# Moving the split of p' w_in from VectorE to ScalarE and GpSimd, from the third batch on

## The chip, the cores and the metric

The kernel runs on one core of a Trainium2 chip. Its engines each follow their own queue of instructions: TensorE (PE in the profile; its weight loads are PEld), VectorE (DVE), ScalarE (ACT), GpSimd (POOL) and SyncE (SP), which here issues the transfers. The metric is the time on the device in microseconds (us). Three runs of the kernel before took 813.12, 812.82 and 815.71 us; the median is 813.12 us.

## The reference

Eight batches of 576 tokens with 8 heads of 64 go through a packed attention, and its output through a feed-forward network (FFN) with a leaky activation, all in float32:

```python
p_packed = sm_attn(p, k, v)                # 32 packed rows per head
out = sm_attn(q, p_packed, p_packed)       # softmax over the 32 packed rows
x = out.transpose(0, 2, 1, 3).reshape(B * S, H * D)
h = x @ w_in                               # (4608, 512) x (512, 2048)
g = np.maximum(h, 0.0) + alpha * np.minimum(h, 0.0)
return g @ w_out                           # (4608, 2048) x (2048, 512)
```

## The kernel before

The attention's output is A times the packed rows p', where A holds the softmax weights of 32 packed rows for each of 8 heads, 256 columns in all. So x w_in is A (p' w_in), and the kernel never forms x: for each batch it computes p' w_in once (256 x 2048) and multiplies A with it. That product is the tile `pw`, kept in float32 in four pieces of 512 columns for each batch.

TensorE multiplies fp32r, a rounded float32. To keep the precision the kernel splits an operand in two: a high part, which is the value cast to fp32r, and a low part, which is the value less the high part, cast too. A product is then three matmuls: high by high, low by high, and high by low.

The FFN goes over half-batches k (288 tokens, two for each batch) and over f, 16 slices of 128 of the 2048 hidden columns. One step is a call of `first` and a call of `second`, two steps apart:

- `first(k, f)` multiplies two halves of `pw` with A into `ps_h` in PSUM (lines 639, 640, 641: high by high, high by A's low part, low by high: six matmuls), and then runs a chain of four small operations: `neg` on ScalarE (645), the leaky sum into `ps_h` on VectorE (646), `gh`, the high part, on ScalarE (651), `gl`, the low part, on VectorE (652).
- `second(k, f)` multiplies `gh` and `gl` with w_out into four accumulators `acc` (669, 670, 671: twelve matmuls).

`split_pw(k, h)` (lines 606 to 616) makes the high part `pwh` and the low part `pwl` of 256 columns of `pw`, which serve two steps f. They have two buffers each. It is called anew for each half-batch, so eight times for each k; k from 2 on needs it (k 0 and 1 go another way), which makes 14 times 8, or 112 calls. For k 2 and 3 (the second batch) ScalarE casts, from k 4 on (the third batch) VectorE casts; VectorE subtracts in all of them.

Beside the FFN of two batches the attention of the next two runs, and then their p' w_in (lines 595 to 597, copied to `pw` at 600, with the split w_in loaded at 567 into `w`, which has three buffers). In the attention GpSimd has the low parts of k and q (`xl`, 180), of v (`vs`, 309, one buffer) and of A (`a_l`, 455), and two steps of the second softmax (431, 438). ScalarE has their high parts (179, 308, 454).

The order of each engine's queue is not written out: a scheduler with its own estimate of every duration sorts the instructions when the kernel is built, and each engine then works through its queue strictly in that order.

Of the kernel before, what the change touches and what calls it, by code (L numbers as in the profile page):

```python
# [13 lines left out]
ALU = mybir.AluOpType  # L14
# [8 lines left out]
def fv(ap):  # L23

    return ap.bitcast(F32)
# [3 lines left out]
def pack_attention_ffn_kernel(  # L29
# [20 lines left out]
    nc = tc.nc  # L50
# [24 lines left out]
    op = ctx.enter_context(tc.tile_pool(name="op", bufs=4))  # L75
# [530 lines left out]
    def split_pw(k, h):  # L606

        src = pw[k // 2, h // 2][:, :, (h % 2) * 256 : (h % 2) * 256 + 256]
        th = pwj.tile([P, 2, 256], F32R, name="pwh", tag="pwh")
        tl = pwj.tile([P, 2, 256], F32R, name="pwl", tag="pwl")  # L610
        if k < 4:
            nc.scalar.copy(out=th, in_=src)  # L612
        else:
            nc.vector.tensor_copy(out=th, in_=src)  # L614
        nc.vector.tensor_tensor(out=tl, in0=src, in1=fv(th), op=ALU.subtract)  # L615
        pj[k, h] = (th, tl)

    def first(k, f):
# [4 lines left out]
        if k < 2 * XF:  # L623
            th, a_f = pw[k // 2, f // 4], result[k // 2]
            fs = slice((f % 4) * P, (f % 4) * P + P)
            for i in range(2):
                nc.tensor.matmul(  # L627
                    ps[:, :HS], th[:, i, fs], a_f[:, i, tok], start=(i == 0), stop=(i == 1)
                )
        else:  # L630
            a_h, a_l = result[k // 2]
            key = (k, f // 2)
            if key not in pj:
                split_pw(*key)
            th, tl = pj[key]
            fs = slice((f % 2) * P, (f % 2) * P + P)
            for i in range(2):
                hi, lo = (i == 0), (i == 1)
                nc.tensor.matmul(ps[:, :HS], th[:, i, fs], a_h[:, i, tok], start=hi, stop=False)  # L639
                nc.tensor.matmul(ps[:, :HS], th[:, i, fs], a_l[:, i, tok], start=False, stop=False)  # L640
                nc.tensor.matmul(ps[:, :HS], tl[:, i, fs], a_h[:, i, tok], start=False, stop=lo)  # L641
# [181 lines left out]
```

## Time and profile before

| what | value |
|---|---|
| median of three runs | 813.12 us |
| the profiled execution | 815.99 us, of it 813.9 us span |
| PE busy | 774.5 us (95%) |
| DVE busy | 611.6 us (75%) |
| ACT busy | 495.1 us (61%) |
| POOL busy | 186.5 us (23%) |
| `pwl` on DVE, line 615, 112 times | 89.9 us, 802 ns each |
| `pwh` on DVE, line 614, 96 times | 53.9 us, 562 ns each |
| `pwh` on ACT, line 612, 16 times | 9.9 us, 618 ns each |

The span is the time from the first to the last instruction of one profiled execution; the execution took 2.1 us more than its span. Busy time of PE counts overlapping matmuls once, so 95% does not say that TensorE had to wait for the other 5% alone. What an engine waits for is named by the semaphore that came last. The chain that ended last goes back from the last instruction, at each step to what released it.

### The profile page before, as it was taken

The page shows a single profiled execution, that of the slowest core. Times are in us where ns is not written, and L with a number is a line of the kernel's source. Part 1 is how long each engine was busy: PE and PEld are TensorE (multiplying, and loading weights), DVE is VectorE, ACT ScalarE, POOL GpSimd, SP SyncE. Part 2 cuts the span into 40 slices and gives each one's busy share as a digit, 9 for nine tenths or more (in the row PEclk, how much of TensorE's full clock was granted, in tenths as well). Part 3 has the DMA queues.
Part 4 walks back from the last instruction along what each step waited for, and adds up shares of the span by engine and source line. Part 5 has one row for each costly group of instructions (what it writes and reads, how often), then busy time and mean ns, then how long its engine had stood idle before and what let it go on. Part 6 is the DMA issues. An engine that isn't in the chain of part 4 may idle for free.

```text
span 813.9 us, 14922 instructions
## 1 busy us (share of the span) xinstructions
PE 774.5 (95%) x5376; PEld 731.0 (90%) x5376; DVE 611.6 (75%) x1302; ACT 495.1 (61%) x1162; POOL 186.5 (23%) x195
## 2 busy tenths in 40 slices
PE   5789999999989899999999999999999999999997
PEld 4557678989989799998999999999999999999997
DVE  4999799778877567899886487898975466666664
ACT  5788898777766676565657655566557533333332
POOL 2101312225436113354342012444311000000000
PEclk9979999999999999999999999999999999999999
DMA  9977787322414743222227522321007200000000
GB/s 298 375 240 241 265 288 246 111 62 59 126 53 128 262 150 97 75 67 66 63 74 230 200 59 59 89 59 45 2 26 260 81 31 1 31 1 30 1 30 30
DMA packets 58457, 93.77 MB, mean 115 GB/s; under 512 B 5136, under 2 KB 36880, under 8 KB 58384
## 3 DMA queue, kind: packets, MB, share of 16 engines
q1 hardware_dynamic: 58384, 92.83, 35.0%
q8 instruction: 42, 0.69, 0.3%
q14 instruction: 31, 0.25, 0.1%
HBM read 72.88 MB, written 19.92 MB: 114 GB/s over the span
## 4 chain that ended last, share of the span: by engine, by line
PE 76%; DVE 9%; DMA 5%; ACT 4%; issue 1%; ACTq 0%; SPq 0%; DVEq 0%
PE acc L669 15%; PE acc L670 14%; PE acc L671 14%; PE ps_h L639 6%; PE ps_h L640 6%; PE ps_h L641 6%; DMA w<-w_split 3%; PE ps_h L627 3%; PE ps_m L595 1%; PE ps_m L216 1%; PE ps_m L597 1%; PE ps_m L596 1%; PE ps_m L217 1%; PE ps_m L350 1%; DVE pwl L615 1%
## 5 line engine op out<-in xcount | busy, mean ns | idle before, releaser
L669 PE MATMUL acc<-gh,wo 128*128 128x288 f32 x1024 | 287.9, 301 | 9.2 <-ACT gh L651 8.2
L670 PE MATMUL acc<-gh,wo 128*128 128x288 f32 x1024 | 282.9, 296 | 0.0
L669 PEld LDWEIGHTS acc<-gh,wo 128*128 128x128 f32 x1024 | 193.0, 189 | 16.3 <-ACT gh L651 12.3
L671 PE MATMUL acc<-gl,wo 128*128 128x288 f32 x1024 | 198.0, 299 | 0.0
L670 PEld LDWEIGHTS acc<-gh,wo 128*128 128x128 f32 x1024 | 193.2, 189 | 1.7 <-issue 0.2
L651 ACT CAST gh<-ps_h 128x288 fp32r<-128x288 f32 x256 | 102.0, 400 | 124.6 <-DVE ps_h L646 122.7
L652 DVE TENSOR_TENSOR gl<-ps_h,gh 128x288 fp32r<-128x288 f32 x256 | 115.5, 453 | 71.8 <-ACT gh L651 70.4
L645 ACT ACTIVATE neg<-ps_h 128x288 f32<-128x288 f32 x256 | 105.4, 412 | 99.5 <-PE ps_h L641 89.5
L646 DVE SCALAR_TENSOR_TENSOR ps_h<-neg,nal,ps_h 128x288 f32<-128x288 f32 x256 | 131.3, 515 | 46.1 <-ACT neg L645 45.5
L671 PEld LDWEIGHTS acc<-gl,wo 128*128 128x128 f32 x1024 | 157.0, 188 | 2.6
L639 PE MATMUL ps_h<-a_h,pwh 128*128 128x288 f32 x448 | 134.2, 300 | 3.4 <-DVE gl L652 3.3
L640 PE MATMUL ps_h<-a_l,pwh 128*128 128x288 f32 x448 | 132.2, 295 | 0.0
L641 PE MATMUL ps_h<-a_h,pwl 128*128 128x288 f32 x448 | 131.9, 295 | 0.0
L180 POOL TENSOR_TENSOR xl<-xraw,xh 128x576 fp32r<-128x576 f32 x48 | 70.0, 1460 | 200.4 <-ACT xh L179 185.8
L615 DVE TENSOR_TENSOR pwl<-pw,pwh 128x512 fp32r<-128x512 f32 x112 | 89.9, 802 | 9.4 <-ACT pwh L612 3.5
L639 PEld LDWEIGHTS ps_h<-a_h,pwh 128*128 128x128 f32 x448 | 84.2, 188 | 6.0 <-DVE gl L652 5.0
L640 PEld LDWEIGHTS ps_h<-a_l,pwh 128*128 128x128 f32 x448 | 84.3, 188 | 0.5
L641 PEld LDWEIGHTS ps_h<-a_h,pwl 128*128 128x128 f32 x448 | 84.2, 188 | 0.1
L600 ACT COPY pw<-ps_m 64x512 f32<-64x512 f32 x120 | 69.6, 580 | 18.5 <-PE ps_m L597 16.6
L614 DVE CAST pwh<-pw 128x512 fp32r<-128x512 f32 x96 | 53.9, 562 | 24.1 <-PE ps_h L640 23.7
L309 POOL TENSOR_TENSOR vs<-vraw,vs 128x640 fp32r<-128x640 f32 x24 | 38.8, 1616 | 40.3 <-ACT vs L308 38.7
L219 ACT COPY lo<-ps_m 64x288 f32<-64x288 f32 x96 | 37.6, 396 | 9.4 <-PE ps_m L217 7.3
(128 smaller groups left out, 987.8 us busy)
## 6 DMA issues: line engine op xcount, KB each, us to landing
w<-w_split SPq DMA_DIRECT2D x48, 512.0 KB, 3.9
xraw<-in_kT SPq DMA_DIRECT2D x32, 288.0 KB, 3.0
xraw<-in_qT SPq DMA_DIRECT2D x32, 288.0 KB, 2.8
outT<-ot SPq DMA_DIRECT2D x64, 144.0 KB, 2.2
vraw<-in_v SPq DMA_DIRECT2D x32, 256.0 KB, 3.0
wraw<-in_w_in SPq DMA_DIRECT2D x16, 512.0 KB, 5.8
wraw<-in_w_out SPq DMA_DIRECT2D x16, 512.0 KB, 4.9
w_split<-w SPq DMA_DIRECT2D x16, 512.0 KB, 3.6
```

What stands on the lines that cost most here:

```text
L180: nc.gpsimd.tensor_tensor(out=xl, in0=raw, in1=fv(xh), op=ALU.subtract)
L615: nc.vector.tensor_tensor(out=tl, in0=src, in1=fv(th), op=ALU.subtract)
L639: nc.tensor.matmul(ps[:, :HS], th[:, i, fs], a_h[:, i, tok], start=hi, stop=False)
L640: nc.tensor.matmul(ps[:, :HS], th[:, i, fs], a_l[:, i, tok], start=False, stop=False)
L641: nc.tensor.matmul(ps[:, :HS], tl[:, i, fs], a_h[:, i, tok], start=False, stop=lo)
L645: nc.scalar.activation(out=neg, in_=x, func=AF.Relu, scale=-1.0)
L646: nc.vector.scalar_tensor_tensor(out=x, in0=neg, scalar=nal[:, f : f + 1], in1=x, op0=ALU.mult, op1=ALU.add)
L651: nc.scalar.copy(out=gh, in_=x)
L652: nc.vector.tensor_tensor(out=gl, in0=x, in1=fv(gh), op=ALU.subtract)
L669: nc.tensor.matmul(acc[o][:, :HS], wo_t[f][:, 0, os_], gh, start=begin, stop=False)
L670: nc.tensor.matmul(acc[o][:, :HS], wo_t[f][:, 1, os_], gh, start=False, stop=False)
L671: nc.tensor.matmul(acc[o][:, :HS], wo_t[f][:, 0, os_], gl, start=False, stop=end)
```

## The change

From k 4 on the cast to `pwh` runs on ScalarE, as it did for k below 4, and the subtraction to `pwl` on GpSimd. VectorE keeps the subtraction for k 2 and 3 alone. Ninety-six casts and 96 subtractions leave VectorE's queue.

```diff
@@ split_pw
-        if k < 4:
-            nc.scalar.copy(out=th, in_=src)
-        else:
-            nc.vector.tensor_copy(out=th, in_=src)
-        nc.vector.tensor_tensor(out=tl, in0=src, in1=fv(th), op=ALU.subtract)
+        nc.scalar.copy(out=th, in_=src)
+        low = nc.vector if k < 4 else nc.gpsimd
+        low.tensor_tensor(out=tl, in0=src, in1=fv(th), op=ALU.subtract)
         pj[k, h] = (th, tl)
```

The file is two lines shorter, so lines from 615 on have numbers lower by two in the rows of the change (646 becomes 644); its cast is line 611 and its subtraction 613. The scheduler sorted all queues anew. Up to the first split of the third batch nothing moved. Three places behind it matter for the prediction. A number behind a name tells the tiles of one name apart.

**First place**, about 408 us into the span, VectorE's queue in the fourth batch's FFN. `s2` and `c` belong to the attention. Before:

```order
L453 STREAM_TRANSPOSE s2_4579<-t1_4693 128x576
L652 TENSOR_TENSOR gl_5601<-ps_h_5586,gh_5600 128x288
L359 TENSOR_TENSOR c_4789<-ps_m_4790,ct_4796 128x128
L614 CAST pwh_5699<-pw_3145 128x512
L615 TENSOR_TENSOR pwl_5700<-pw_3145,pwh_5699 128x512
L646 SCALAR_TENSOR_TENSOR ps_h_5616<-neg_5623,nal_107,ps_h_5616 128x288
L652 TENSOR_TENSOR gl_5627<-ps_h_5616,gh_5626 128x288
```

Now:

```order
L650 TENSOR_TENSOR gl_5601<-ps_h_5586,gh_5600 128x288
L436 TENSOR_SCALAR z2_4744<-z2_4744 128x18
L437 RECIPROCAL z2_4744<-z2_4744 128x18
L644 SCALAR_TENSOR_TENSOR ps_h_5616<-neg_5623,nal_107,ps_h_5616 128x288
L359 TENSOR_TENSOR c_4789<-ps_m_4790,ct_4796 128x128
L650 TENSOR_TENSOR gl_5627<-ps_h_5616,gh_5626 128x288
L644 SCALAR_TENSOR_TENSOR ps_h_5642<-neg_5653,nal_107,ps_h_5642 128x288
L453 STREAM_TRANSPOSE s2_4579<-t1_4693 128x576
```

Nothing of the split stands between two steps of the FFN's chain any more, and the attention's transpose has gone two steps back. ScalarE's queue at the same place, before:

```order
L651 CAST gh_5600<-ps_h_5586 128x288
L358 COPY ct_4796<-ps_m_4790 128x128
L308 CAST vs_4799<-vraw_4724 128x5x128
L454 CAST a_h_4822<-s2_4579 128x576
L645 ACTIVATE neg_5623<-ps_h_5616 128x288
L651 CAST gh_5626<-ps_h_5616 128x288
```

Now:

```order
L649 CAST gh_5600<-ps_h_5586 128x288
L611 CAST pwh_5699<-pw_3145 128x512
L643 ACTIVATE neg_5623<-ps_h_5616 128x288
L358 COPY ct_4796<-ps_m_4790 128x128
L308 CAST vs_4799<-vraw_4724 128x5x128
L649 CAST gh_5626<-ps_h_5616 128x288
```

The cast of the split stands right ahead of `neg`.

**Second place**, about 529 us, GpSimd's queue in the fifth batch's FFN, at the k and q of the next attention. Before:

```order
L438 TENSOR_TENSOR t1_6782<-t1_6782,z2_6831 128x576
L409 CAST pt_110<-p2_109 128x2x64 x2
L180 TENSOR_TENSOR xl_6850<-xraw_6680,xh_6849 128x576
L455 TENSOR_TENSOR a_l_6866<-s2_6663,a_h_6865 128x576
L180 TENSOR_TENSOR xl_7125<-xraw_7017,xh_7124 128x576
```

Now:

```order
L438 TENSOR_TENSOR t1_6782<-t1_6782,z2_6831 128x576
L613 TENSOR_TENSOR pwl_7414<-pw_5328,pwh_7413 128x512
L188 MEMSET vraw_7259 64x128
L409 CAST pt_110<-p2_109 128x2x64 x2
L455 TENSOR_TENSOR a_l_6866<-s2_6663,a_h_6865 128x576
L180 TENSOR_TENSOR xl_6850<-xraw_6680,xh_6849 128x576
L613 TENSOR_TENSOR pwl_7488<-pw_5328,pwh_7487 128x512
L180 TENSOR_TENSOR xl_7125<-xraw_7017,xh_7124 128x576
```

`xl_6850` has moved behind a `pwl` and behind `a_l`. TensorE's queue where it is read, before:

```order
L671 MATMUL acc3_7131<-gl_7215,wo4_558 128x288
L216 MATMUL ps_m_6876<-xh_6849,s1_108 128x288
L217 MATMUL ps_m_6870<-xl_6850,s1_108 128x288
L217 MATMUL ps_m_6876<-xl_6850,s1_108 128x288
L669 MATMUL acc0_7128<-gh_7273,wo5_658 128x288
```

Now:

```order
L669 MATMUL acc3_7131<-gl_7331,wo6_725 128x288
L216 MATMUL ps_m_6876<-xh_6849,s1_108 128x288
L217 MATMUL ps_m_6870<-xl_6850,s1_108 128x288
L217 MATMUL ps_m_6876<-xl_6850,s1_108 128x288
L667 MATMUL acc0_7128<-gh_7367,wo7_938 128x288
```

The reader has moved too: from behind f 4 (`wo4`) to behind f 6 (`wo6`), two steps of the FFN later.

**Third place**, about 270 us, SyncE's queue at the start of the third batch's FFN. `w` is a piece of the split w_in, `outT` a part of the output. Before:

```order
L567 DMA w_3378<-w_split_100 128x1024
L567 DMA w_3398<-w_split_100 128x1024
L687 DMA outT<-ot_3579 128x288
L687 DMA outT<-ot_3585 128x288
L567 DMA w_3450<-w_split_100 128x1024
```

Now:

```order
L567 DMA w_3378<-w_split_100 128x1024
L685 DMA outT<-ot_3579 128x288
L685 DMA outT<-ot_3585 128x288
L567 DMA w_3398<-w_split_100 128x1024
L685 DMA outT<-ot_3591 128x288
L567 DMA w_3450<-w_split_100 128x1024
```

Two writes of the output have moved ahead of the load of `w_3398`.

## The prediction

> **What bounds the kernel now.** I read the busy time of each engine first, then the same by stages, then who TensorE waits for, and last the chain of waits at the places where it stood still.
>
> ```profile
> span 813.9 us, 14922 instructions
> PE 774.5 (95%) x5376; PEld 731.0 (90%) x5376; DVE 611.6 (75%) x1302; ACT 495.1 (61%) x1162; POOL 186.5 (23%) x195
> ```
>
> The stages, with PE, PEld, DVE, ACT and POOL busy, their instructions, the granted clock, and the transfers:
>
> ```profile
> 268.00:281.00 13.00, 9.67 (x49) 8.50 (x50) 7.77 (x15) 8.49 (x17) 1.45 (x2) 0.91 0.84 274
> 345.00:380.00 35.00, 32.87 (x242) 31.79 (x241) 33.09 (x65) 21.17 (x52) 16.21 (x16) 1.00 0.23 69
> 405.00:415.00 10.00, 8.87 (x69) 8.73 (x68) 8.51 (x17) 4.78 (x12) 4.74 (x5) 1.00 0.11 31
> 495.00:535.00 40.00, 38.46 (x283) 36.97 (x282) 34.25 (x72) 23.38 (x59) 16.39 (x17) 1.00 0.23 68
> 281.00:780.00 499.00, 493.05 (x3611) 483.55 (x3610) 365.17 (x762) 273.96 (x651) 104.67 (x97) 1.00 0.24 76
> 720.00:780.00 60.00, 60.00 (x456) 60.00 (x454) 38.87 (x80) 21.88 (x55) 0.00 (x0) 1.00 0.06 21
> ```
>
> TensorE is the bound. From 720 to 780 us it never stops: 60.00 us for 456 matmuls is 132 ns each, and a step of 18 matmuls takes 2.37 us. The first changed split starts at about 268 us, so nothing before that can move. From 281 to 780 us TensorE stands idle for 499.00 - 493.05 = 5.95 us, of it 2.13 us in 345 to 380, 1.13 in 405 to 415 and 1.54 in 495 to 535: 4.80 us in three stretches where VectorE is 95%, 85% and 86% busy. That is nearly all that a lighter VectorE can give back. Whom TensorE waited for between 281 and 780 us (total us, times, longest one):
>
> ```profile
> PE acc L669 <- ACT gh L651: 3.3, 4, 1.1
> PE ps_m L595 <- DMA w<-w_split: 1.2, 2, 0.7
> PE acc L669 <- DVE ot L685: 0.7, 2, 0.4
> PE ps_m L216 <- DVE p L385: 0.5, 1, 0.5
> PE ps_h L639 <- DVE gl L652: 0.3, 1, 0.3
> ```
>
> All but the transfer's 1.2 us end with the FFN's chain or VectorE: 8 waits, 4.8 us. The name `gh` is ScalarE's, but ScalarE was late because VectorE was. The chain that ended last shows it at 408 us (start, us, what), and at 530 us likewise:
>
> ```profile
> 409.26 1.57 DVE pwh L614
> ...
> 410.93 1.73 DVE pwl L615
> 412.65 0.44 DVE ps_h L646
> ...
> 413.12 0.41 ACT gh L651
> ...
> 413.57 0.40 PE acc L669
> ```
>
> ```profile
> 529.89 1.67 DVE pwh L614
> ```
>
> At 408 us the split alone holds the chain for 3.3 us. A cast of 1.57 or 1.67 us is not what it usually costs. GpSimd at the same time:
>
> ```profile
> 408.97 1.57 POOL L309 TENSOR_TENSOR vs<-vraw,vs 128x640 fp32r<-128x640 f32 x1 [1.06 <-ACT vs L308]
> 410.50 1.61 POOL L455 TENSOR_TENSOR a_l<-s,a_h 128x576 fp32r<-128x576 f32 x1
> ```
>
> VectorE's cast ends just after GpSimd's first subtraction does (410.83 and 410.54), and `pwl` just after the second (412.66 and 412.11). They hold each other up.
>
> **The change part by part.** VectorE's groups between 281 and 814 us (busy us, mean ns, then idle before and what ended it), with ScalarE's and GpSimd's groups nearest to the new operations, from 60 us on:
>
> ```profile
> L646 DVE SCALAR_TENSOR_TENSOR ps_h<-neg,nal,ps_h 128x288 f32<-128x288 f32 x190 | 97.6, 516 | 41.7 <-ACT neg L645 41.3
> L615 DVE TENSOR_TENSOR pwl<-pw,pwh 128x512 fp32r<-128x512 f32 x93 | 74.3, 798 | 5.7 <-PE ps_h L641 0.4
> L614 DVE CAST pwh<-pw 128x512 fp32r<-128x512 f32 x93 | 52.7, 567 | 24.1 <-PE ps_h L640 23.7
> L612 ACT CAST pwh<-pw 128x512 fp32r<-128x512 f32 x16 | 9.9, 618 | 3.7 <-PE ps_h L640 3.6
> L180 POOL TENSOR_TENSOR xl<-xraw,xh 128x576 fp32r<-128x576 f32 x48 | 70.0, 1460 | 200.4 <-ACT xh L179 185.8 <-PE ps_h L640 9.5 <-PE ps_h L641 2.8
> L309 POOL TENSOR_TENSOR vs<-vraw,vs 128x640 fp32r<-128x640 f32 x24 | 38.8, 1616 | 40.3 <-ACT vs L308 38.7 <-PE ps_h L627 1.0 <-PE acc L671 0.6
> ```
>
> *Removed.* VectorE loses 52.7 + 74.3 = 127 us, so its 365 us between 281 and 780 become some 240 of 499: half busy. What that is worth is not 127 us but the waits of TensorE. By the three stretches it is 4.80 us; since a matmul is busy for 295 ns but a new one starts every 132, each of the 8 waits hides another 0.16 us, and the ceiling is 4.80 + 8 x 0.16 = 6.1 us. At 408 us the split was 3.3 us of a chain that came 1.1 us late, so without it the wait is gone. I take four fifths for what is really regained, since the order is new and some waits will stand elsewhere: **-4.9 us**. The bounds are nothing and -6.1.
>
> *Added to ScalarE.* 93 casts of 618 ns are 57 us, so 274 us of 499 become 331, or 66%. The cast stands ahead of `neg` and waits, as VectorE's did, until `ps_h`'s second high matmul (640) has freed the buffer. What that does is seen in the steady stage, where a split falls into every second step:
>
> ```profile
> 743.79 0.43 DVE L614 CAST pwh<-pw 128x512 fp32r<-128x512 f32 x1 [0.42 <-PE ps_h L640]
> 744.33 0.69 DVE L615 TENSOR_TENSOR pwl<-pw,pwh 128x512 fp32r<-128x512 f32 x1
> 744.94 0.52 DVE L646 SCALAR_TENSOR_TENSOR ps_h<-neg,nal,ps_h 128x288 f32<-128x288 f32 x1
> 743.99 0.41 ACT L645 ACTIVATE neg<-ps_h 128x288 f32<-128x288 f32 x1 [1.11 <-PE ps_h L641]
> 745.49 0.40 ACT L651 CAST gh<-ps_h 128x288 fp32r<-128x288 f32 x1 [1.08 <-DVE ps_h L646]
> 746.64 0.30 PE L669 MATMUL acc<-gh,wo 128*128 128x288 f32 x1
> ```
>
> Before, `neg` was done at 744.40 and `ps_h` still waited for `pwl` until 744.94. Now the cast ends at 743.79 + 0.62 = 744.41, `neg` at 744.82, and `ps_h` can start at 744.86: 0.08 us earlier. `gh` is needed at 746.64 and was there at 745.89. So in the steady stage the cast costs **nothing**, hidden by the slack of 0.75 us; were that slack gone, each cast would cost up to 0.45 us of lateness of `neg`. Beside the attention, where ScalarE has long casts too, I charge +0.2 us.
>
> *Added to GpSimd.* No row has 128x512 there. From 1460 ns for 576 columns and 1616 for 640, 64 columns are worth 156 ns, and 512 take about 1.30 us; the bounds are VectorE's undisturbed 0.69 (row at 744.33) and 1.46. 93 of them are 121 us, so 105 us of 499 become 226, or 45%. They are covered by time: a split made at 743.79 takes the buffer that one pair of steps just freed and serves the pair after the running one, two steps or 4.7 us later. Cast and subtraction took 0.43 + 0.69 = 1.1 us and now take 0.62 + 1.30 = 1.9, which leaves 2.8 us, room for one long subtraction of the attention ahead in GpSimd's queue and not for two.
>
> *GpSimd's own work made later.* `xl_6850` now waits behind a `pwl` and `a_l` (second place in the order), about 1.3 + 1.6 us. Its reader on TensorE has been moved back by two steps, 4.7 us. I charge nothing.
>
> *What VectorE still shares with GpSimd.* The tiny scalar operation on `z` swings likewise (ns, least, median, most):
>
> ```profile
> L436 DVE TENSOR_SCALAR z<-z x16: 127/168/1398, 32.3 to 612.1; 128x18 f32<-128x18 f32 x16
> ```
>
> `ps_h`, which reads PSUM, takes 516 ns in the mean and 0.52 us in the steady stage with GpSimd idle, so it is not held. With GpSimd busy twice as long, `z` meets it more often: 8 of them after 281 us at up to 1.2 us more each, of which TensorE sees a part: +0.5 us, between 0 and 2. The Trainium skill (SBUF — State Buffer, "Who interferes with whom") says that a two-input VectorE operation on SBUF and the faster modes of copies and scalar operations exclude a GpSimd operation for its whole length, whichever starts first; the trace agrees in the casts of 1.57 and 1.67 us. By that rule the removed operations are the very ones that were held, so all 6.1 us would come back, and the sum would be -4.9 us.
>
> *Transfers.* At the third place `w_3398` is now issued behind two output writes. It is what TensorE waits for there:
>
> ```profile
> 271.90 5.65 DMA w<-w_split
> ```
>
> ```profile
> 272.32 0.86 SPq L687 DMA_DIRECT2D outT<-ot  x2
> ```
>
> The stage 268 to 281 lost 13.00 - 9.67 = 3.3 us so. The two writes took 0.86 us to issue and were ready before, so the load goes out at most that much later, and less where they no longer wait behind it: +0.5 us, between 0 and 0.9.
>
> The sum is -4.9 + 0.2 + 0.5 + 0.5 = **-3.7 us**. The profiled execution took 815.99 us (813.9 span and 2.1 around it) and would take 812.3, with a span of 810.2. It lies 2.9 us above the median of the runs, which the sum does not explain; I take the same difference off the median: 813.12 - 3.7 = **809.4 us**.
>
> **The rivals.**
>
> *The waits come back elsewhere.* The queues follow the scheduler's estimates, not the chip's times, and ScalarE at 66% takes VectorE's place as the engine that comes late where the attention is dense. For it: ScalarE's queue at 408 us now has two of the attention's operations, `ct` and `vs`, between `neg` and `gh`. Against it: ScalarE stays less busy than VectorE's 73% was, and its rows do not swell beside GpSimd. A quarter of the gain is left, -1.2 us: 811.9 us.
>
> *ScalarE's queue makes it slower.* The cast holds `neg` until line 640 is done and 0.62 us more, in every second step. It decides where `gh` has under 0.45 us of slack, and the waits above say that there is none at some places beside the attention. If each of the 46 splits between 345 and 600 us (93 over 516 us are one in 5.5) lost 0.2 us, that is +9 us, and with the gain +4 to +5: 818 us. Against it is the working of the steady stage, where the lateness of `neg` was already paid by `pwl`.
>
> *GpSimd is late.* `vs` has one buffer, so TensorE soon waits for it, and it now queues behind a `pwl` whose cast may not have come: each of the 8 attention calls from 281 us on (4 batches, two calls each) makes two, and if the first of each is 1.3 us late, that is 8 x 1.3, or +10 us, with the gain +5: 818 us. It decides where `vs` ends later than TensorE arrives. Against it: GpSimd is idle over half the time, and the one reader that the order shows (`xl_6850`) was moved back by more than the delay. The Trainium skill (GPSIMD Engine Reference, "Engine selection") keeps two-input elementwise work on VectorE, as GpSimd takes about twice as long; the rows agree, with 1.46 us for 576 columns on GpSimd against 0.69 for 512 on VectorE.
>
> **How the numbers follow.** A run can be told from no change at about 0.5%, or 4.1 us: below 809.1 is faster, above 817.2 slower. The forecast has 0.56 (own range 807 to 811), the waits that come back 0.30, ScalarE slower 0.08, GpSimd late 0.06. The forecast's centre lies 0.3 us above the bound, and its terms are more likely too small than too large in the gain; I give faster 0.45, of which nearly all is the forecast's, same 0.43, and slower 0.12, the last two rivals less their milder forms. The range takes the ceiling of 6.1 with a little of the transfers' 3.3 at the lower end, 806 us, and half of the way to the slower rivals at the upper, 815.
>
> **What would show it.** Right: `pwl` on GpSimd at 1.2 to 1.4 us, `pwh` on ScalarE at 0.62; VectorE's busy time near 480 us; idle time of TensorE between 281 and 780 us at 1 to 3 us, with no wait of over 0.5 us on `gh`. Wrong: waits of lines 217, 350 or, in the new file's count, 639 (for `xl`, `vs` and `pwl`) on GpSimd; `gh` behind ScalarE's cast; or a stage 268 to 281 that loses over 4.5 us.

## The result: 1.1% faster, more than twice the gain that was forecast

| | kernel before | changed kernel |
|---|---|---|
| median | 814.41 us (4 runs, 812.82 to 818.53) | 805.40 us (4 runs, 804.80 to 808.08) |
| profiled execution | 815.99 us, span 813.9 | 805.65 us, span 803.9 |

The ratio is 0.9892, with a 95% interval of 0.9868 to 0.9917. The forecast was 809.4 us with a range of 806 to 815; the time lies 4.0 us below the one and 0.6 below the other. Measured again beside the experiments, the changed kernel had a median of 807.24 us against 814.84, a ratio of 0.9911 (0.989 to 0.9931). The direction was right and the size was not: -10.3 us in the profiled executions, where the sum had -3.7.

### The profile page after: what moved, and what is told of

Read it like the earlier page. It is cut to its first block, busy times and chain, and to the rows that moved or that the text cites. A ratio compares the mean times of both kernels' runs of the same rounds, so it can differ in the third digit from the quotient of the medians.

```text
span 803.9 us, 15166 instructions
## 1 busy us (share of the span) xinstructions
PE 769.7 (96%) x5376; PEld 729.5 (91%) x5376; DVE 500.7 (62%) x1110; ACT 544.9 (68%) x1258; POOL 305.6 (38%) x291
## 4 chain that ended last, share of the span: by engine, by line
PE 83%; DVE 6%; ACT 3%; DMA 2%; issue 1%; SPq 0%; ACTq 0%; DVEq 0%
PE acc L667 16%; PE acc L669 16%; PE acc L668 15%; PE ps_h L637 7%; PE ps_h L638 7%; PE ps_h L639 7%; PE ps_h L625 3%; PE ps_m L350 2%; PE ps_m L595 2%; PE ps_m L216 2%; PE ps_m L597 1%; PE ps_m L596 1%; PE ps_m L217 1%; PE ps_m L328 1%; PE ps_m L212 1%
## 5 line engine op out<-in xcount | busy, mean ns | idle before, releaser
L613 POOL TENSOR_TENSOR pwl<-pw,pwh 128x512 fp32r<-128x512 f32 x96 | 124.1, 1293 | 217.9 <-ACT pwh L611 183.2
L669 PE MATMUL acc<-gl,wo 128*128 128x288 f32 x1024 | 201.5, 299 | 0.0
L611 ACT CAST pwh<-pw 128x512 fp32r<-128x512 f32 x112 | 69.4, 620 | 61.9 <-PE ps_h L638 60.5
```

Source lines behind the costliest of these rows:

```text
L613: low.tensor_tensor(out=tl, in0=src, in1=fv(th), op=ALU.subtract)
L669: nc.tensor.matmul(acc[o][:, :HS], wo_t[f][:, 0, os_], gl, start=False, stop=end)
```

## The profile after

The page's first lines of the changed kernel:

```profile
span 803.9 us, 15166 instructions
PE 769.7 (96%) x5376; PEld 729.5 (91%) x5376; DVE 500.7 (62%) x1110; ACT 544.9 (68%) x1258; POOL 305.6 (38%) x291
```

The stages of the changed kernel, with the same columns as before (length, then PE, PEld, DVE, ACT and POOL busy with their instructions, the granted clock, the share of the transfers and their GB/s):

```profile
268.00:281.00 13.00, 10.58 (x63) 8.95 (x62) 5.36 (x13) 11.64 (x23) 6.40 (x5) 1.00 0.90 302
281.00:780.00 499.00, 497.39 (x3683) 491.59 (x3682) 265.17 (x593) 324.54 (x750) 217.86 (x188) 1.00 0.25 76
345.00:380.00 35.00, 35.00 (x269) 35.00 (x268) 23.06 (x56) 25.83 (x63) 24.34 (x23) 1.00 0.25 74
405.00:415.00 10.00, 10.00 (x78) 10.00 (x78) 5.15 (x14) 6.41 (x15) 8.60 (x8) 1.00 0.11 31
495.00:535.00 40.00, 39.60 (x302) 39.37 (x301) 27.20 (x65) 28.16 (x70) 25.10 (x25) 1.00 0.26 73
```

TensorE now stands idle for 1.61 us of the 499, where it was 5.95. The three stretches of which the prediction spoke lose 0.40 us instead of 4.80. Whom TensorE waited for between 281 and 780 us is now two lines instead of five:

```profile
PE acc L667 <- ACT gh L649: 1.2, 1, 1.2
PE ps_h L637 <- DVE gl L650: 0.4, 1, 0.4
```

The idle time is only part of it. A weight load that waits lets the matmul ahead of it run on, so that PE still counts as busy. The group of the weight loads of `gh` between 282 and 814 us, before (busy us and mean ns, then the idle time ahead of them and what ended it), and the same group of the changed kernel:

```profile
L669 PEld LDWEIGHTS acc<-gh,wo 128*128 128x128 f32 x764 | 143.4, 188 | 7.4 <-ACT gh L651 5.2 <-DVE ot L685 0.6 <-ACT vs L308 0.5
```

```profile
L667 PEld LDWEIGHTS acc<-gh,wo 128*128 128x128 f32 x764 | 143.4, 188 | 2.3 <-ACT gh L649 1.4
```

Here 5.1 us of idle time went, 3.8 of it in waits for `gh`; the waits of the matmuls themselves for `gh` had shown 3.3 before and 1.2 now.

To see where in the kernel the time went, I took the starts of TensorE's matmuls by their number in its queue. Number 1489 lies just ahead of the first changed split, number 1570 some 3 us behind the stage 268 to 281:

| | before | after | difference |
|---|---|---|---|
| up to matmul 1489 (nothing changed there) | 266.1 us | 268.1 us | +2.0 |
| 1489 to 1570 | 18.8 us | 15.9 us | -2.9 |
| 1570 to the end | 524.4 us | 515.2 us | -9.2 |

The first two rows nearly cancel: number 1570 starts at 284.9 us before and at 284.1 now. In a second profile of the changed kernel the last row is 515.4 us, so it repeats. A start is late by as much as its distance from the one ahead of it exceeds the usual distance, 0.13 us for 288 columns. Of the -9.2 us, starts that came over 0.3 us late make up -5.6 (10 of them with 7.5 us before, 2 with 1.9 now), those that came 0.12 to 0.3 us late -0.8 (5 before, none now), and those under 0.12 us late -2.4 (53 before with 4.8 us, 28 now with 2.4). The remaining 0.4 are spread over the regular starts. The starts under 0.12 us late are the part that PE's busy time hides.

The new operations, on GpSimd and ScalarE, between 282 and 814 us:

```profile
L613 POOL TENSOR_TENSOR pwl<-pw,pwh 128x512 fp32r<-128x512 f32 x93 | 120.3, 1293 | 212.8 <-ACT pwh L611 178.1 <-PE acc L669 15.6 <-PE ps_h L639 11.7
L611 ACT CAST pwh<-pw 128x512 fp32r<-128x512 f32 x93 | 57.7, 620 | 58.2 <-PE ps_h L638 57.0 <-POOL xl L180 1.0
```

## The experiments

The theory after the result: the split's two operations on VectorE and GpSimd's subtractions of the attention held each other up, and the change ended these **meetings**. The rivals: VectorE simply had **too much work** between two steps of the FFN's chain, whoever else was running; or the scheduler's new **order at the start** of the third batch made the gain. All ratios are to the kernel before, whose median lay between 814.37 and 814.84 us beside every group. Work that an experiment adds is read by nothing.

### Each half of the change alone

The cast to ScalarE alone, the subtraction stays on VectorE:

```diff
 nc.scalar.copy(out=th, in_=src)
-low = nc.vector if k < 4 else nc.gpsimd
-low.tensor_tensor(out=tl, in0=src, in1=fv(th), op=ALU.subtract)
+nc.vector.tensor_tensor(out=tl, in0=src, in1=fv(th), op=ALU.subtract)
```

> Half of the change: from the third batch on the cast to pwh runs on ScalarE, the subtraction to pwl stays on VectorE. Theory V (TensorE was held by VectorE's queue, so the gain goes with what leaves it): 52.7 of VectorE's 127 us leave, about two fifths of the gain of 9 us, so 0.9955 of before, 809 to 812 us; TensorE still waits at gh at some places, for pwl is still held by GpSimd. Theory O (the gain comes from the new order of the queues and the transfers at the start of the third batch, not from VectorE's load): no relation to the share removed; either all of the 1.1% or none.

Measured: 809.86 us, 0.9941 (0.9921 to 0.996).

The subtraction to GpSimd alone, VectorE casts:

```diff
-nc.scalar.copy(out=th, in_=src)
+if k < 4:
+    nc.scalar.copy(out=th, in_=src)
+else:
+    nc.vector.tensor_copy(out=th, in_=src)
```

> The other half: from the third batch on VectorE casts as before and GpSimd subtracts. Theory V: 74.3 of 127 us leave VectorE, which would be three fifths of the gain (0.9935, about 809 us), but the casts that stay meet GpSimd more often, so their mean rises above 567 ns, towards 0.8 us, and the gain falls to a third or a half (0.994 to 0.997). Theory O: no relation; all or none.

Measured: 809.66 us, 0.9939 (0.9917 to 0.9961). Each half gives 0.6%, and the two add up to about the whole, 1.1%. What stayed on VectorE still swelled at times. The subtraction in the first kernel and the cast in the second, least, median and most ns of 93:

```profile
L612 DVE TENSOR_TENSOR pwl<-pw,pwh x93: 622/693/1910, 284.6 to 790.8; 128x512 fp32r<-128x512 f32 x93
```

```profile
L614 DVE CAST pwh<-pw x93: 384/428/1824, 284.9 to 791.0; 128x512 fp32r<-128x512 f32 x93
```

Both the load and the meetings were halved here, so this tells nothing between the two.

### The start of the third batch alone, and all but the start

The change for the first four splits of the third batch only:

```diff
-nc.scalar.copy(out=th, in_=src)
-low = nc.vector if k < 4 else nc.gpsimd
+start = k == 4 and h < 4
+if k < 4 or start:
+    nc.scalar.copy(out=th, in_=src)
+else:
+    nc.vector.tensor_copy(out=th, in_=src)
+low = nc.gpsimd if start else nc.vector
```

The other kernel makes the change for all but these four:

```diff
-if k < 4 or start:
+if k < 4 or not start:
...
-low = nc.gpsimd if start else nc.vector
+low = nc.vector if k < 4 or start else nc.gpsimd
```

> The change for the first four splits of the third batch alone (k 4, h 0 to 3). In the traces the stage from the last units of p' w_in before the third batch to its second step took 18.8 us before and 15.9 after, and TensorE's clock was 0.91 and 1.00 in it. If that part of the gain belongs to the split's engines at that place: 2 to 3 us less, 0.996 to 0.998, with a clock of 1.00 in 268 to 281 us. If it is only the later order of the whole rest: 0.999 to 1.001.

> The change for all splits from the third batch on but the first four. If the start stage is worth 2 to 3 us by itself: 0.992 to 0.994, the stage at 18 to 19 us. If not: as the change, 0.989 to 0.991.

Measured: 814.93 us, 1.0011 (0.9994 to 1.0029), for the start alone, and 806.17 us, 0.9905 (0.989 to 0.992), for all but the start. The start gives nothing and the rest gives all: the theory of the order at the start falls. The -2.9 us between matmuls 1489 and 1570 in the profiled pair are then no part of the gain that repeats. The profile of the start alone shows what became of them: it took 16.1 us there, as the change did, but came to matmul 1489 at 268.7 us, and so to 1570 at 284.7, all but as before. The section on the hardware comes back to this.

### The split's work put back on VectorE beside the change

The changed kernel, with VectorE casting and subtracting once more right behind `pwh`, at the same time as GpSimd's subtraction:

```diff
+if k >= 4:
+    nc.vector.tensor_copy(out=dh, in_=fv(th))
+    nc.vector.tensor_tensor(out=dl, in0=src, in1=fv(th), op=ALU.subtract)
```

> The changed kernel, and in addition VectorE casts and subtracts again behind each of the 96 splits, into tiles that nobody reads any more. So the real split is off VectorE, but VectorE's queue is as full as before, with operations that GpSimd excludes. Theory V: back to before, 0.997 to 1.003 (812 to 817 us), the added cast and subtraction swelling to 0.6 and 0.8 us in the mean. Theory O: stays at the changed kernel's 0.989 to 0.992.

In its twin two reductions of `pwh` stand at the same place:

```diff
+if k >= 4:
+    nc.vector.tensor_reduce(out=dr, in_=fv(th)[:, :, :144], axis=AX.X, op=ALU.max)
+    nc.vector.tensor_reduce(out=ds, in_=fv(th), axis=AX.X, op=ALU.max)
```

> As the run before it, with the same positions in VectorE's queue, but the two added operations are reductions of 288 and 512 elements of pwh: about as long when undisturbed (0.43 and 0.68 us), and reductions did not swell beside GpSimd in the trace of before (0.74 us alone and with it). What they leave out is only the meeting of the two engines. If VectorE's plain load is the cause: as the run before it, 0.997 to 1.003. If the holding up by GpSimd is the cause: near the changed kernel, 0.989 to 0.993. Between, if both: 0.994.

Measured: 892.44 us, 1.0969 (1.0937 to 1.1001), and 821.45 us, 1.0099 (1.0073 to 1.0125). VectorE's and GpSimd's groups between 282 and 814 us (first kernel), and one place of its timeline on VectorE and on GpSimd:

```profile
L620 DVE TENSOR_TENSOR ptf<-pw,pwh 128x512 fp32r<-128x512 f32 x82 | 133.8, 1632 | 0.0
L619 DVE CAST s1f<-pwh 128x512 fp32r<-128x512 f32 x83 | 56.0, 675 | 51.2 <-ACT pwh L611 50.3
```

```profile
709.52 0.43 DVE L619 CAST s1f<-pwh 128x512 fp32r<-128x512 f32 x1 [1.87 <-ACT pwh L611]
709.86 1.78 DVE L620 TENSOR_TENSOR ptf<-pw,pwh 128x512 fp32r<-128x512 f32 x1
```

```profile
709.57 1.53 POOL L613 TENSOR_TENSOR pwl<-pw,pwh 128x512 fp32r<-128x512 f32 x1 [4.58 <-ACT pwh L611]
```

GpSimd's subtraction ends at 711.10 us; VectorE's, which takes 0.69 us undisturbed, ends 0.54 us later, at 711.64: most of its own work came when GpSimd's was done. The mean of 1632 ns says that it is so in nearly every split, and between 281 and 780 us TensorE waits 45 times for the `gh` that comes behind it, 40.8 us in all. The twin's reductions do not swell, but they wait for ScalarE's cast at the head of VectorE's queue, and the row shows it:

```profile
L617 DVE TENSOR_REDUCE dr<-pwh 128x2 f32<-128x288 f32 x93 | 41.8, 449 | 72.5 <-ACT pwh L611 71.9
```

So the meeting costs 71 us where it happens in nearly every split. No theory had expected either kernel to be slower than the first one by as much as 1%. The twin's own +1.0% holds a wait for another engine beside the plain load, so the load was still without a price.

To take that wait away, the same operations were given the `pwh` of the split before this one (`before`, kept from the last call). First a cast and a subtraction, then, in the twin, the two reductions:

```diff
+if k >= 4:
+    before = fv(last[0])
+    nc.vector.tensor_copy(out=dh, in_=before)
+    nc.vector.tensor_tensor(out=dl, in0=before, in1=fv(dh), op=ALU.subtract)
+last[:] = [th]
```

> The changed kernel; in addition VectorE casts and subtracts 128x512 for each of the 96 splits, but reads the high part of the split before, which has long been there. So nothing waits for ScalarE's cast, as it did in e3_again, and the added work does not start together with GpSimd's subtraction. Theory V (load and meetings of VectorE): VectorE is as busy as before the change, so 0.997 to 1.005. If the 1.097 of e3_again came from starting together with GpSimd each time, the added subtraction falls from 1.64 us to 0.8 to 1.0 us here. If the plain wait for ScalarE made e3_again slow, the same fall in time, but the subtraction stays as long.

> As e5_prev_shared, with reductions of 288 and 512 elements of the split before in place of the cast and the subtraction (0.45 and 0.68 us, which GpSimd does not hold). It is VectorE's plain load, without meetings and without a wait for ScalarE. If the load alone took the gain: 0.997 to 1.003. If the meetings or the place in the queue did: 0.989 to 0.993, and then the 1.010 of e4_unshared was its wait for ScalarE's cast.

Measured: 824.56 us, 1.0141 (1.0121 to 1.0161), and 822.43 us, 1.0106 (1.0092 to 1.0121). This separation failed: the scheduler put the operations right behind the cast that they read, one split earlier, so that VectorE waited for ScalarE as in the pair above. The reductions' row of the twin:

```profile
L619 DVE TENSOR_REDUCE dr<-pwh 128x2 f32<-128x288 f32 x93 | 41.8, 449 | 72.7 <-ACT pwh L611 72.1
```

The twin repeats the run with reductions, and the pair says no more than that meetings at this place add some 0.35%, with intervals that touch.

### Plain work on VectorE that waits for nobody

The changed kernel, with three reductions of `gl` right behind `gl` (which VectorE has made itself), in every second step:

```diff
+if k >= 4 and f % 2 == 0:
+    for i, n in enumerate((HS, HS, HS // 2)):
+        nc.vector.tensor_reduce(out=dr[i], in_=fv(gl)[:, :n], axis=AX.X, op=ALU.max)
```

> The changed kernel with work added to VectorE that waits for no other engine and is not of the kind that GpSimd's subtraction met in the run with the repeated split: behind `gl` of every second step from the third batch on VectorE takes the maximum of 288, 288 and 144 elements of each of `gl`'s rows (96 times three reductions, about 0.45 + 0.45 + 0.23 us by the 449 ns of the same operation in the run with two reductions; the results are read by nothing). That is about 108 us, nearly the 127 us that the split took there before. If VectorE's load by itself was what the change took away, the gain goes: ratio 0.997 to 1.005. If the meetings with GpSimd and the place between two steps of the chain were the cause, the load is hidden: ratio 0.988 to 0.994, VectorE busy near 605 us.

In its twin nearly the same load is made of the split's kinds of operation:

```diff
+if k >= 4 and f % 2 == 0:
+    nc.vector.tensor_tensor(out=d0, in0=fv(gl), in1=fv(gh), op=ALU.subtract)
+    nc.vector.tensor_tensor(out=d1, in0=fv(gl), in1=fv(gh), op=ALU.subtract)
+    nc.vector.tensor_copy(out=d0, in_=fv(gl))
```

> The same place behind `gl` and nearly the same load as in the run with three reductions, but of the kinds that the split has: two subtractions gl - gh of 288 columns and a cast of 288 (96 times, results read by nothing). If only VectorE's load counts, it takes the same time as its twin with reductions, within 0.3%. If meetings with GpSimd count, it is slower than its twin by 0.5% or more, since GpSimd is busy for 306 us in all: ratio to the kernel before 0.997 to 1.01, and the mean of the subtractions lies well above 0.45 us, as does GpSimd's mean for `pwl` above 1.29 us.

Beside them the changed kernel unaltered:

> The changed kernel unaltered, as the baseline of its three neighbours on the same chip and with more rounds. Ratio 0.987 to 0.992; TensorE idle between 281 and 780 us for 1 to 3 us; the start stage (matmul 1489 to 1570) at 16 to 18.5 us, by whether TensorE's clock is halved after its wait there.

Measured: 815.75 us, 1.0009 (0.9993 to 1.0025), with reductions; 843.53 us, 1.0358 (1.0332 to 1.0383), with subtractions; 807.24 us, 0.9911 (0.989 to 0.9931), without either. The groups of the kernel with reductions and of the one with subtractions:

```profile
L655 DVE TENSOR_REDUCE dr<-gl 128x1 f32<-128x288 f32 (+1 forms) x285 | 97.1, 395 | 2.6
```

```profile
L657 DVE TENSOR_TENSOR ptf<-gl,gh 128x288 fp32r<-128x288 f32 x91 | 68.1, 748 | 0.0
L656 DVE TENSOR_TENSOR s1f<-gl,gh 128x288 fp32r<-128x288 f32 x91 | 53.4, 587 | 2.4
L658 DVE CAST s1f<-gl 128x288 fp32r<-128x288 f32 x91 | 53.2, 585 | 0.1
```

Both theories have a price here. Work that never swells gives the whole gain back, which spoke for the load, although the longest single waits of TensorE in that profile are for transfers (3.3 us in two between 281 and 780 us). Work that swells costs 28 us more, with the first and the second subtraction, which are alike, at 587 and 748 ns in the mean against medians of 459 and 452. Which of the two had held the kernel before was still open, for in it the load lay elsewhere, ahead of `ps_h`, and GpSimd had less to do.

### Taking the meetings away from the kernel before

This pair decides. In the kernel before, and in the changed one, the attention's subtractions of k, q, v and A on GpSimd are left out from the fifth batch's attention on, which is the one that runs beside the FFN from 281 us. The split stays whole on VectorE in the first, and its load with it. TensorE's matmuls keep their number; they read the high part in place of the low one (`split_x` has a new argument `low`):

```diff
-split = (lambda x: x) if exact else split_x
+split = (lambda x: x) if exact else (lambda x: split_x(x, b < 4))
...
+if not low:
+    return xh, xh
...
-a_l = at.tile([P, 2, S], F32R, name="a_l", tag="a_l")
+a_l = at.tile([P, 2, S], F32R, name="a_l", tag="a_l") if b < 4 else a_h
+if b < 4:
     nc.gpsimd.tensor_tensor(
         out=vs[:, :, 1, :], in0=vraw[i], in1=fv(vs[:, :, 0, :]), op=ALU.subtract
     )
...
-pc[:, : 2 * P], aT[:, kt, i], vs[:, kt],
+pc[:, : 2 * P], aT[:, kt, i], vs[:, kt] if b < 4 else vs[:, kt, 0:1].broadcast_to([P, 2, P]),
...
+if b < 4:
     nc.gpsimd.tensor_tensor(out=a_l[:, tp, :], in0=s2, in1=fv(a_h[:, tp, :]), op=ALU.subtract)
```

> The kernel before, with three quarters of GpSimd's work beside the FFN from the third batch on left out: from the fifth batch's attention on (which runs there) the low parts of k, q, v and A are not computed, and TensorE multiplies the high part in their place, so its count of matmuls stays. The split stays whole on VectorE. GpSimd's 105 us between 281 and 780 us become some 28, and VectorE's load stays at some 350 us. If the meetings of VectorE with GpSimd were what the change took away, this kernel gains as much: ratio 0.987 to 0.993, `pwl` on VectorE near 0.70 us in the mean and the cast near 0.45. If VectorE's load by itself was it, ratio 0.996 to 1.002, although both means fall. Some gain, to 0.997, can come from low parts that TensorE no longer waits for; the twin run shows how much.

> The changed kernel with the same low parts left out. It shows what leaving them out is worth where VectorE has no split: by both theories little, ratio 0.986 to 0.992 to the kernel before. The difference to its twin is the answer: under 0.3% if meetings were the cause of the gain, 0.6 to 1% if the load was.

Measured: 805.86 us, 0.9894 (0.9872 to 0.9916), for the kernel before without these subtractions, and 805.70 us, 0.9891 (0.9869 to 0.9914), for the changed one without them. Where GpSimd hardly meets it, the split costs nothing on VectorE that these runs can show: the change is then worth 0.03%, with intervals of 0.2% on either side, and the changed kernel gains nothing clear over what it had (0.9892 and 0.9911 with the subtractions). GpSimd's lateness for its own readers was not it either: TensorE's listed waits between 281 and 780 us, in the kernel before and in the changed one, name GpSimd nowhere. The stage of the kernel before without these subtractions:

```profile
281.00:780.00 499.00, 498.91 (x3693) 492.83 (x3692) 351.42 (x778) 276.90 (x659) 26.49 (x45) 1.00 0.24 75
```

VectorE is busy for 351 of the 499 us, all but as long as before (365), and TensorE idles for 0.09 us, less than in the changed kernel. The split's rows in the kernel before, and in it without these subtractions (least, median and most ns):

```profile
L614 DVE CAST pwh<-pw x93: 356/427/1798, 284.8 to 796.3; 128x512 fp32r<-128x512 f32 x93
L615 DVE TENSOR_TENSOR pwl<-pw,pwh x93: 671/692/1911, 285.8 to 796.8; 128x512 fp32r<-128x512 f32 x93
```

```profile
L618 DVE CAST pwh<-pw x93: 384/427/1067, 282.8 to 783.9; 128x512 fp32r<-128x512 f32 x93
L619 DVE TENSOR_TENSOR pwl<-pw,pwh x93: 650/692/1544, 283.6 to 784.4; 128x512 fp32r<-128x512 f32 x93
```

```profile
L619 DVE TENSOR_TENSOR pwl<-pw,pwh 128x512 fp32r<-128x512 f32 x93 | 67.7, 728 | 6.4 <-DVE pwh L618 0.5 <-PE acc L675 0.5
L618 DVE CAST pwh<-pw 128x512 fp32r<-128x512 f32 x93 | 40.5, 436 | 26.6 <-PE ps_h L644 26.3
```

The medians are the same. The means fall from 567 to 436 ns and from 798 to 728 ns, which for 93 of each is 12.2 + 6.5 = 18.7 us. Few splits make up the whole: 18 of the 93 casts in the kernel before took over 600 ns, and 3 in this one.

Equal times alone would not show that the same waits went, since these kernels leave TensorE next to nothing to wait for, and every kernel's queues were sorted anew. The trace of the kernel before shows it. Between matmul 1570 and the end, eight starts that wait for no transfer come over 0.3 us late, 6.1 us in all. Seven of them, with 5.7 us, end a chain with an operation on VectorE in it that took two to seven times its median while GpSimd worked: casts and subtractions of the split before those at 353.8, 376.1, 379.0, 413.6, 520.2 and 534.3 us, and `z` with 1162 ns before the one at 374.7. Only the eighth, at 503.5 us with 0.4, has none ahead of it.

What was left was the load behind `gl`, which had cost the whole gain. The same reductions without GpSimd's subtractions:

> The changed kernel with the attention's low parts left out from the fifth batch on (as in its twin without the low parts) and with the three reductions behind `gl` of every second step on VectorE. With the attention's GpSimd work in place these reductions gave the whole gain back (ratio 1.0009). If VectorE's load of 108 us at that place costs by itself, it does so here too: ratio 0.997 to 1.002. If it costs only where the rest of VectorE's and GpSimd's work meets, the load is hidden as the split's own was in the kernel before without low parts: ratio 0.987 to 0.992.

Measured: 812.19 us, 0.9959 (0.9945 to 0.9973), between the two answers. Against its baseline of 0.9891 the load behind `gl` costs 0.7% without the attention's subtractions, and 1.0% with them (1.0009 against 0.9911). Plain load can cost, then, at a place where the split did not stand before. In this kernel's profile the waits of TensorE between 281 and 780 us are mostly for a transfer:

```profile
PE ps_m L599 <- DMA w<-w_split: 2.0, 1, 2.0
PE acc L675 <- ACT gh L653: 0.4, 2, 0.3
```

Why 100 us of work are free ahead of `ps_h` and not behind `gl`, and how much of it is the transfers' new places in SyncE's queue, stays open.

### The change from the second batch on

The one candidate for more: the split leaves VectorE in the second batch too.

```diff
-low = nc.vector if k < 4 else nc.gpsimd
-low.tensor_tensor(out=tl, in0=src, in1=fv(th), op=ALU.subtract)
+nc.gpsimd.tensor_tensor(out=tl, in0=src, in1=fv(th), op=ALU.subtract)
```

> A candidate: the split is ScalarE's cast and GpSimd's subtraction from the second batch on too (k 2 and 3, 16 more subtractions). If lightening VectorE is the cause and GpSimd has room there, it gains a share of 16/96 of what the subtraction alone gave (0.6%), about 0.1%: ratio 0.987 to 0.990. If GpSimd's attention work stands ahead of it at that place, 0.990 to 0.995.

Measured: 817.08 us, 1.0027 (1.0005 to 1.0048), so 1.2% slower than the change, which neither expectation covered. The stage 100 to 180 us, in which the second batch's FFN begins, in this kernel and in the changed one measured beside it:

```profile
100.00:180.00 80.00, 72.58 (x470) 66.12 (x468) 65.07 (x134) 66.13 (x146) 31.30 (x24) 0.98 0.53 180
```

```profile
100.00:180.00 80.00, 75.51 (x498) 68.87 (x497) 69.33 (x151) 67.42 (x151) 19.33 (x16) 1.00 0.55 182
```

TensorE loses 3 us more and gets 28 matmuls less far; up to matmul 1489 it took 274.9 us instead of 266.4, and from 1489 to 1570 20.6 instead of 17.7. TensorE's waits for `gh` between 100 and 200 us are 5.4 us in 4 instead of 2.5 in 3, the longest, of 2.7 us, ahead of the matmul at 151.8. Which late operation is behind them was not followed further. No kernel tried that keeps all low parts is clearly faster than the change.

## Why the prediction was right and wrong

**The mechanism was right.** The prediction read the casts of 1.57 and 1.67 us as VectorE and GpSimd holding each other up, and took the waits that followed as what the change removes. It did not part this from the load, and spoke of what "a lighter VectorE can give back". The run without GpSimd's subtractions parts them: 0.9894 with the split and its load left on VectorE, so the meetings are the gain, and the load at that place is not. The sentence from the Trainium skill (SBUF — State Buffer, "Who interferes with whom") held as well, and its result, -4.9 us, was nearer than the forecast: reductions did not swell (395 ns), and two-input subtractions and casts of data in SBUF did (587, 748 and 585 ns in the mean against medians of 459, 452 and 304).

**The step that failed is *Removed*, the ceiling of 4.80 + 8 x 0.16 = 6.1 us and the four fifths of it.** From matmul 1570 on the changed kernel measured -9.2 us in the profiled pair, with the costs of the other terms already in it. The ceiling was made from PE's idle time in three stretches. There the reading was nearly exact, 4.40 of 4.80 us regained. But it left out what lies outside the stretches and below the threshold of a listed wait. Starts that came less than 0.12 us late gave 2.4 us, and the weight loads' busy time had shown that something was missing: between 281 and 780 us PE gained 4.34 us of busy time (493.05 to 497.39), and PEld 8.04 (483.55 to 491.59). The Trainium skill (Perfetto Trace Analysis, "Identifying the Most-Contended Engine") says that the matmuls' busy time is a bad measure of TensorE's headroom and names the weight loads' among those to take instead; here the one came to about half of the 9.2 us and the other to nearly nine tenths. The two waits for transfers at 451 and 613 us, 1.5 us by the late starts, which the text set aside as not VectorE's, went as well; why is not shown. The discount of a fifth had no row behind it.

**Transfers, +0.5, had the wrong sign in the profiled pair** (-2.9 us there, or -0.9 with the +2.0 ahead of it) **and no effect that repeats**: the change at the start alone gave 1.0011.

**The charge of +0.5 for `z` was wrong.** GpSimd is busy twice as long between 281 and 780 us, and yet `z` no longer swells at all (it had 1398 ns at most). Why the two no longer meet was not followed:

```profile
L436 DVE TENSOR_SCALAR z<-z x16: 128/168/177, 31.5 to 607.9; 128x18 f32<-128x18 f32 x16
```

**ScalarE's and GpSimd's added work were right.** `pwl` takes 1293 ns (1.30 was worked out), `pwh` 620 (618), and nothing of TensorE waits for `pwl` or `xl`. The Trainium skill's advice against GpSimd for two-input work (GPSIMD Engine Reference, "Engine selection") is borne out in the duration, 1293 ns against 692, and the move still gains 0.6%, since nobody waits. The steady stage is the one worked out, on ScalarE and on VectorE:

```profile
743.34 0.62 ACT L611 CAST pwh<-pw 128x512 fp32r<-128x512 f32 x1 [0.85 <-PE ps_h L638]
743.87 0.40 ACT L643 ACTIVATE neg<-ps_h 128x288 f32<-128x288 f32 x1
744.86 0.40 ACT L649 CAST gh<-ps_h 128x288 fp32r<-128x288 f32 x1 [0.59 <-DVE ps_h L644]
```

```profile
744.30 0.52 DVE L644 SCALAR_TENSOR_TENSOR ps_h<-neg,nal,ps_h 128x288 f32<-128x288 f32 x1 [1.32 <-ACT neg L643]
```

`gh` starts 1.52 us after the cast, against 1.70 before: 0.18 us earlier where 0.08 was worked out, because rows on one engine overlap by some 0.09 us (the cast's 0.62 us end behind the start of `neg`). The same overlap, by estimate some 17 us over the 186 rows that left, accounts for VectorE's busy time falling by 111 us to 500.7 and not to near 480.

**The rivals.** Waits that come back elsewhere were two, 1.37 us at 395.69 (for `gh`, so the "no wait of over 0.5 us on `gh`" was wrong) and 0.56 at 498. ScalarE's queue and GpSimd's lateness did not slow the kernel. The range ended at 806 because it rested on the same ceiling of 6.1 us; the measured 9.2 in its place would have put that end some 3 us lower.

## What to carry to other kernels

Where an operation's mean lies far above its median, look at what its neighbour engine does during the few long ones: that tail, and not the engine's busy time, may be what the bound engine waits for, and leaving out the neighbour's work in one run tells the two apart. For the ceiling of a gain, take the delays from the starts of the bound engine's instructions, or at least from its weight loads, and not from its idle time. An engine that is twice as slow can be the right one for work that nobody waits for, until there is a place where somebody does (the second batch may be one; its late operation was not found).

## What the hardware showed that was not expected

A meeting lengthens the operations on both sides. Starting together in nearly every split, VectorE's subtraction took 1.63 us in the mean instead of 0.69 and GpSimd's 1.53 instead of 1.29 at the place shown, and the kernel became 71 us longer than with reductions in their place.

The stage 268 to 281 runs at two speeds with one and the same program. The changed kernel, measured again:

```profile
268.00:281.00 13.00, 10.61 (x55) 9.44 (x56) 4.20 (x9) 10.65 (x21) 5.51 (x5) 0.89 0.91 297
```

PE is busy for as long as in the first profile (10.58 us), with a granted clock of 0.89 instead of 1.00 and 55 matmuls instead of 63; matmuls 1489 to 1570 took 17.7 us instead of 15.9. In the kernel before the clock there was 0.91, and they took 18.8. The slower stage costs nothing here: both profiles of the changed kernel start matmul 1570 at 284.1 us, for the one that was slower in the stage had come to it earlier (266.4 us against 268.1). What holds both to the same moment was not followed. TensorE waits for a transfer in this stage each time, 1.7 us at the longest in the first profile of the change, 1.8 in the second and 2.7 before, and the clock behind it is not always the same. The Trainium skill (TensorE: Matmul & The Clock Gate, "Part 1: The HAM clock gate") tells of a halved clock after a window of idleness of about 3.4 us; the single waits here were shorter, and no run shows what decides.
